# A 7-product (Strassen) first matrix product over pairs of batches, with its weights streamed from DRAM

## The chip, the cores and the metric

The kernel runs on one core of a Trainium2 chip. A core has a matrix engine (TensorE, `PE` in the profile, with its weight loads as `PEld`), three engines for element-wise work (VectorE `DVE`, ScalarE `ACT`, GpSimd `POOL`) and a sync engine (`SP`) that issues the transfers between DRAM and the on-chip memory SBUF. Matmuls write to PSUM, a second on-chip memory of eight banks. The metric is the device time of one execution in microseconds (us). Before the change the median of three runs was 1854.67 us (1854.55 to 1856.01).

## What is computed

Attention with RMS-normalised queries and keys over 8 batches, 12 heads, 448 positions and 64 columns a head, and behind it a feed-forward layer whose activation is the square of a Relu:

```
q_n, k_n = rmsnorm(q, g_q), rmsnorm(k, g_k)
scores = (1/sqrt(64)) * q_n @ k_n^T
attn = exp(scores - max); attn = attn / (sum(attn) + 1e-9)
x = (attn @ v), heads side by side        # 3584 x 768
h = x @ w_in                              # 768 x 2048
out = relu(h)^2 @ w_out                   # 2048 x 768
```

Inputs q, k, v and the gains are taken as f32. The weights arrive as 64-bit floats; the kernel itself turns their words into f32.

## The kernel before

The kernel has two versions of the work behind a test on the gains; the one with bounded scores (no row maximum), `attention_then_ffn_bounded`, runs here.

**Attention** goes by pairs of heads, 6 pairs a batch, 48 in all. For pair i, `load` and `load_v` (L414, L421) bring q, k and v into SBUF, `norm` (L429) squares on GpSimd (L434), reduces on VectorE (L437), takes the power -1/2 on GpSimd (L439) and scales (L441). `transposes` (L448) turns q and k on TensorE into `pt`, two PSUM tiles of the pool `ps_m`, and VectorE copies them out with the gains (L456). `scores` (L459) makes one of four chunks of keys: two matmuls, one per head, on halves of the array, then an exponential on ScalarE (L468); GpSimd adds the four chunks' probabilities up (L472, L474). `values` (L478) multiplies by v into `pav`; `finish` (L487) forms the row sums `tot` by a matmul with ones (L492), takes the reciprocal on VectorE (L494) and scales `pav` into the tile `xT` (L497).

**Feed-forward** of one batch (`feed_forward`, L506) has 16 row blocks of the first product, each six matmuls `ph` over the 768 inner rows (L513), a Relu on ScalarE (L516) and a square on GpSimd (L517) into `gT`; and then the second product, 128 rows of output at a time, in two halves of 384 columns, each 16 matmuls `po` (L525), copied out by VectorE (L528) or ScalarE (L530) and stored by SP (L533, L535). `ps_m` has two banks, which `pt`, `ph` and `po` share; `pav` and `tot` have one each, the scores four.

**The weights** `w1` and `w2` lie in SBUF throughout. They come in 32 pieces of 128x768, three in flight; `round_weights` (L392) makes f32 of each with five VectorE operations (L402, L404, L405, L407, L408), two on ScalarE (L403, L406) and a product on GpSimd (L409). Raw words and scratch lie in `gT`.

**The order.** The main loop (L560 to L596) goes over the batches; each batch's attention has twelve half-pairs, and after each half-pair some yields of the feed-forward of the batch before are run, so that TensorE has work of both. Batch 0 has no feed-forward to weave in; its half-pairs take the weight pieces instead. The last feed-forward runs alone. TensorE's instructions keep the order in which the program writes them (L635); the other engines' and SP's order is set by the planner, which works with estimated durations. An f32 matmul appears as two records in the profile.

## Time and profile before

| what | value |
|---|---|
| median of three runs | 1854.67 us |
| the profiled execution, its own time | 1852.34 us |
| its span, first to last instruction | 1850.5 us |
| TensorE busy | 1624.2 us (88%) |
| VectorE, ScalarE, GpSimd busy | 496.7, 304.4, 833.4 us |
| mean granted TensorE clock | 0.944 of full speed |
| moved by DMA | 70.16 MB, 38 GB/s on average |

The page cuts the span into 40 slices of 46 us and gives the busy share of an engine in tenths (9 is 90% or more). A table of windows gives the same for chosen stretches. A row of the timeline or of the groups names the line, the operation, output and inputs, partitions x elements, and a count; in a group, `| busy us, mean ns | idle us before it`, with the releaser that ended most of the idle time behind `<-`. The busy time of VectorE and GpSimd includes time in which an instruction has started and is held up.

### The profile page before, as it was taken

What the parts mean: (1) busy time and instruction counts of PE and PEld (TensorE: products, weight loads), DVE (VectorE), ACT (ScalarE), POOL (GpSimd) and SP (SyncE); (2) the same over time, 40 slices, a digit from 0 to 9 for tenths busy, and PEclk for the clock granted to TensorE, in tenths of its full rate; (3) what the DMA queues carried; (4) which work ended last, traced back from release to release, by engine and by line L of the source; (5) the groups of instructions that cost most, each with busy time, mean ns of one, the idle gap of its engine ahead of it and who ended that gap; (6) DMA issues with size and microseconds to landing.
All of it is one profiled execution on the core that took longest, in us unless ns stands there. A gap on an engine that the chain in (4) does not pass through costs nothing.

```text
span 1850.5 us, 13250 instructions
## 1 busy us (share of the span) xinstructions
PE 1624.2 (88%) x5440; PEld 804.5 (43%) x5440; DVE 496.7 (27%) x432; ACT 304.4 (16%) x413; POOL 833.4 (45%) x553
## 2 busy tenths in 40 slices
PE   3242479998999899998999899998999899999998
PEld 1111134454445444454445454454445454455555
DVE  6898941211211211211211212211211212210000
ACT  2333322101120011201120011201120011200100
POOL 6777676622662236622662236622663235601200
PEclk9657679998999999999999999999999999999999
DMA  5433400000100100000100100000100100000000
GB/s 157 135 119 116 148 25 25 20 33 24 30 25 24 37 24 21 25 33 24 30 26 24 37 24 17 29 32 24 30 25 24 37 24 15 10 18 9 0 10 27
DMA packets 47754, 70.16 MB, mean 38 GB/s; under 512 B 3652, under 2 KB 35908, under 8 KB 47684
## 3 DMA queue, kind: packets, MB, share of 16 engines
q1 hardware_dynamic: 47684, 69.22, 12.0%
q8 instruction: 44, 0.72, 0.2%
q14 instruction: 26, 0.21, 0.0%
HBM read 58.20 MB, written 11.01 MB: 37 GB/s over the span
## 4 chain that ended last, share of the span: by engine, by line
PE 81%; POOL 4%; DVE 2%; ACT 1%; issue 0%; POOLq 0%; ACTq 0%
PE po L525 32%; PE ph L513 32%; PE sc L465 7%; PE pav L484 6%; PE tot L492 2%; POOL acc L474 2%; PE pt L454 1%; POOL rstd L439 1%; ACT gT L516 1%; POOL qkn L441 1%; POOL qkn L434 1%; DVE rstd L437 0%; DVE w L407 0%; ACT osb L530 0%; DVE w L408 0%
## 5 line engine op out<-in xcount | busy, mean ns | idle before, releaser
L513 PE MATMUL ph<-xT,w 128*128 128x448 f32 x1536 | 595.6, 544 | 7.6 <-DVE xT L497 7.6
L525 PE MATMUL po<-w,gT 128*128 128x384 f32 x1792 | 592.3, 492 | 0.0
L525 PEld LDWEIGHTS po<-w,gT 128*128 128x128 f32 x1792 | 342.5, 192 | 256.0 <-issue 27.5
L513 PEld LDWEIGHTS ph<-xT,w 128*128 128x128 f32 x1536 | 287.5, 190 | 314.1 <-issue 305.6
L494 DVE RECIPROCAL rec<-tot 128x448 f32<-128x448 f32 x48 | 141.9, 2956 | 554.5 <-PE tot L492 554.5
L517 POOL TENSOR_TENSOR gT<-gT 128x448 f32<-128x448 f32 x128 | 118.3, 933 | 293.9 <-ACT gT L516 293.9
L465 PE MATMUL sc<-qkT 64*112 64x448 f32 x768 | 188.5, 614 | 60.1 <-DVE qkT L456 60.1
L472 POOL TENSOR_TENSOR acc<-pr 112x896 f32<-112x896 f32 x48 | 102.8, 2141 | 287.3 <-ACT pr L468 287.1
L474 POOL TENSOR_TENSOR acc<-acc,pr 112x896 f32<-112x896 f32 x96 | 201.1, 2095 | 27.5 <-ACT pr L468 27.1
L468 ACT ACTIVATE pr<-sc 112x896 f32<-112x896 f32 x192 | 166.9, 913 | 157.5 <-PE sc L465 157.5
L434 POOL TENSOR_TENSOR qkn<-qk 112x1024 f32<-112x1024 f32 x48 | 91.5, 1907 | 201.9 <-PE pt L454 191.7
L516 ACT ACTIVATE gT<-ph 128x448 f32<-128x448 f32 x128 | 69.7, 544 | 596.4 <-PE ph L513 596.4
L484 PE MATMUL pav<-pr,vt 112*64 112x448 f32 x768 | 167.4, 561 | 0.0
L456 DVE TENSOR_SCALAR qkT<-pt,gains 128x448 f32<-128x448 f32 x96 | 65.3, 682 | 340.0 <-PE pt L454 338.9
L454 PE MATMUL pt<-ident,qkn 112*128 112x112 f32 x384 | 62.1, 289 | 98.0 <-POOL qkn L441 88.5
L439 POOL TENSOR_TENSOR rstd<-rstd,mhalf 112x16 f32<-112x16 f32 x48 | 139.7, 2911 | 3.8
L465 PEld LDWEIGHTS sc<-qkT 64*112 64x112 f32 x768 | 67.1, 189 | 141.8 <-issue 133.5
L530 ACT COPY osb<-po 128x384 f32<-128x384 f32 x28 | 13.4, 479 | 682.3 <-PE po L525 682.3
L528 DVE COPY osb<-po 128x384 f32<-128x384 f32 x28 | 15.6, 558 | 349.2 <-PE po L525 349.2
L441 POOL TENSOR_TENSOR qkn<-qk,rstd 112x512 f32<-112x512 f32 x96 | 101.7, 1063 | 3.6
L454 PEld LDWEIGHTS pt<-ident,qkn 112*128 112x128 f32 x384 | 45.3, 153 | 132.2 <-POOL qkn L441 83.0
L484 PEld LDWEIGHTS pav<-pr,vt 112*64 112x64 f32 x768 | 48.3, 139 | 115.1 <-issue 90.2
(27 smaller groups left out, 497.4 us busy)
## 6 DMA issues: line engine op xcount, KB each, us to landing
gT<-in_moe_w_in_dram SPq DMA_DIRECT2D x16, 768.0 KB, 4.8
gT<-in_moe_w_out_dram SPq DMA_DIRECT2D x16, 768.0 KB, 4.3
qk<-in_q_dram SPq DMA_DIRECT2D x48, 224.0 KB, 2.9
qk<-in_k_dram SPq DMA_DIRECT2D x48, 224.0 KB, 3.2
vt<-in_v_dram SPq DMA_DIRECT2D x48, 224.0 KB, 2.7
out_dram<-osb SPq DMA_DIRECT2D x24, 384.0 KB, 2.3
out_dram<-osb SPq DMA_DIRECT2D x8, 192.0 KB, 2.7
gains<-in_g_q_dram SPq DMA_DIRECT2D x2, 0.2 KB, 2.9
```

The lines of the kernel that those rows point to most:

```text
L434: nc.gpsimd.tensor_tensor(sq, flat, flat, ALU.mult)
L439: nc.gpsimd.tensor_tensor(rflat, rflat, mhalf, ALU.pow)
L441: nc.gpsimd.tensor_tensor(qkn[:, s].rearrange("p j h d -> p h j d"), qk[:, s].rearrange("p h (j d) -> p h j d", d=D), rstd[:, s].rearrange ...
L454: nc.tensor.transpose(pt[:, j * SP:(j + 1) * SP], qkn[:, s, j].rearrange("p h d -> p (h d)"), ident[:SP, :SP])
L465: nc.tensor.matmul(sc[:, h, 0:S], qkT[rows, 1, c * SP:(c + 1) * SP], qkT[rows, 0, :], start=True, stop=True)
L468: nc.scalar.activation(pr, sc[:, :, 0:S], AF.Exp)
L474: nc.gpsimd.tensor_tensor(accs[i], accs[i], pr, ALU.add)
L484: nc.tensor.matmul(pavs[i][h * D:(h + 1) * D, :], vs[i][:, h, c, :], pr[:, h, :], start=(c == 0), stop=(c == NJ - 1))
L494: nc.vector.reciprocal(rec, tot)
L513: nc.tensor.matmul(ph, w1[:, c, f * P:(f + 1) * P], xT[:, c, :], start=(c == 0), stop=(c == NPAIR - 1))
L517: nc.gpsimd.tensor_tensor(g, g, g, ALU.mult)
L525: nc.tensor.matmul(po, gT[:, f, c0 + t:c0 + t + P], w2[:, f, cols], start=(f == 0), stop=(f == NFC - 1))
```

## The change

Attention itself keeps its shape; the feed-forward now takes two batches (896 rows) at a time, four such *spans*.

- **First product.** The 2 x 2 block product (inner halves of 384, row blocks f and f + 8 of the 2048, the two batches) is made with seven block products in place of eight (`first_product`). The seven combinations of weight blocks of each f are computed once, on GpSimd, and stored in a DRAM tile `w1s`; in each span they are loaded again, 192 KB each, six buffers, five products ahead (`load_blocks`). The combinations of the inputs are made by VectorE in `finish` (`xC`, and part of `xT`). Seven products are combined through PSUM accumulation (`pa`, `pd`, `pc` are each reopened once) and VectorE additions.
- **Second product.** It goes over 896 rows in seven tiles, yields after every matmul, and takes the 16 blocks in an order that leaves the last written ones to the end.
- **Order.** Head: attention of batches 0 and 1 with the conversion of w_in (`make_w1`). Then, four times, the first product alone, and the second product woven with the attention of the next two batches. w_out is converted (`make_w2`) during the first of the first products.
- **Conversion.** One `min` moves from VectorE to ScalarE: three VectorE operations and an exponent step, three on ScalarE; the fraction's words are overwritten in place.
- **Attention.** The square moves to ScalarE, and so does the evacuation of `pt`; in the head the row sums come from TensorE chunk by chunk (`pe_sums`) with no additions; later one of three additions is on VectorE.
- **SP** now keeps the written order too.

```diff
+    HC = NPAIR // 2
+    HF = NFC // 2
+    NSPAN = B // 2
...
+    gT = consts.tile([P, NFC, 2 * S], F32, name="gT")
+    xT = consts.tile([P, 2, NPAIR, S], F32, name="xT")
+    xC = consts.tile([P, 3, HC, S], F32, name="xC")
+    clamp1 = consts.tile([P, 1], F32, name="clamp1")
...
+    def exponents(words, w):
+        wu = w.bitcast(U32)
+        nc.vector.tensor_scalar(wu, pairs_of(words)[1], 20, 0x7FF, ALU.logical_shift_right, ALU.bitwise_and)
+        nc.scalar.activation(w, wu, AF.Relu, bias=clamp1, scale=-1.0)
+        nc.scalar.activation(wu, w, AF.Relu, bias=clamp2, scale=-(2.0 ** 23))
+    def fractions(words, w):
+        low, high = pairs_of(words)
+        wu = w.bitcast(U32)
+        f = low.bitcast(F32)
+        nc.vector.scalar_tensor_tensor(wu, high, 0x80000000, wu, ALU.bitwise_and, ALU.bitwise_or)
+        nc.vector.tensor_scalar(high, high, 0xFFFFF, None, ALU.bitwise_and)
+        nc.vector.scalar_tensor_tensor(f, low, 2.0 ** -32, high, ALU.mult, ALU.add)
+        nc.scalar.activation(f, f, AF.Copy, bias=1.0, scale=2.0 ** -20)
...
+    w1s = dram.tile([HF, 7, P, HC * P], F32, name="w1s")
+    SETS = 3
...
+    def make_w1(n, step):
+        if not 0 <= n < NFC:
+        b = [w1_blocks(n)[:, i] for i in range(8)]
+        at = (S2, A22)[n % 2]
+        e = w1_blocks(n)[:, at:at + 2].rearrange("p k m -> p (k m)")
+        words = w1_words(n)
+        A21 = 7
+        if step == 0 and doubles:
+            exponents(words, e)
+        if step == 1 and doubles:
+            fractions(words, e)
+        if step == 2:
+            for half, blk in enumerate(((A11, A12), (A21, A22))[n % 2]):
+                part = slice(half * HC * P, (half + 1) * HC * P)
+                if doubles:
+                    nc.gpsimd.tensor_tensor(b[blk], pairs_of(words)[0].bitcast(F32)[:, part], e[:, part], ALU.mult)
+                else:
+                    nc.gpsimd.tensor_copy(b[blk], words.bitcast(F32)[:, part])
+            load_w1(n + SETS)
+        if step == 2 and n % 2:
+            nc.gpsimd.tensor_tensor(b[S1], b[A21], b[A22], ALU.add)
+            nc.gpsimd.tensor_tensor(b[S2], b[S1], b[A11], ALU.subtract)
+            nc.gpsimd.tensor_tensor(b[S3], b[A11], b[A21], ALU.subtract)
+            nc.gpsimd.tensor_tensor(b[S4], b[A12], b[S2], ALU.subtract)
+        if step == 3 and n % 2:
+            nc.sync.dma_start(w1s[n // 2].rearrange("k p m -> p k m"), w1_blocks(n)[:, 0:7])
...
+    def w2_words(n):
+        f = (HF - 2, NFC - 2, HF - 4)[n % SETS]
+        return gT[:, f:f + 2, :].rearrange("p f n -> p (f n)")[:, 0:2 * NW].bitcast(U32)
...
+    def make_w2(n, step):
+        if not 0 <= n < NFC:
+            return
+        if step == 0 and doubles:
+            exponents(w2_words(n), w2[:, n])
+        if step == 1 and doubles:
+            fractions(w2_words(n), w2[:, n])
+        if step == 2:
+            if doubles:
+                f = pairs_of(w2_words(n))[0].bitcast(F32)
+                nc.gpsimd.tensor_tensor(w2[:, n], f, w2[:, n], ALU.mult)
+            load_w2(n + SETS)
+    stream = []
+    def load_blocks(upto):
+        while len(stream) < min(upto, NSPAN * HF * 7):
+            n = len(stream)
+            sw = loads.tile([P, HC, P], F32, tag="sw", name="sw", bufs=6)
+            nc.sync.dma_start(sw.rearrange("p c m -> p (c m)"), w1s[n // 7 % HF, n % 7])
+            stream.append(sw)
...
     def norm(i):
         qk = qks.pop(i)
...
-        nc.gpsimd.tensor_tensor(sq, flat, flat, ALU.mult)
+        nc.scalar.activation(sq, flat, AF.Square)
...
     def transposes(i):
         qkn = normed.pop(i)
...
-            nc.vector.tensor_scalar(qkT[:, s], pt, gains[:, s:s + 1], None, ALU.mult)
+            nc.scalar.activation(qkT[:, s], pt, AF.Copy, scale=gains[:, s:s + 1])
...
         probs[i, c] = pr
-        if c == 1:
+        if c == 0 or pe_sums:
+            pass
+        elif c == 1:
             accs[i] = work.tile([SP, 2, S], F32, tag="acc", name="acc")
             nc.gpsimd.tensor_tensor(accs[i], probs[i, 0], pr, ALU.add)
-        elif c > 1:
-            nc.gpsimd.tensor_tensor(accs[i], accs[i], pr, ALU.add)
+        else:
+            (nc.vector if c == 2 else nc.gpsimd).tensor_tensor(accs[i], accs[i], pr, ALU.add)
         if c == NJ - 1:
             del qkTs[i]
-    def values(i, cs):
+    def values(i, cs, pe_sums):
...
             for h in range(2):
                 nc.tensor.matmul(pavs[i][h * D:(h + 1) * D, :], vs[i][:, h, c, :], pr[:, h, :],
                                  start=(c == 0), stop=(c == NJ - 1))
-    def finish(i):
+            if pe_sums:
+                sums(i, pr, c == 0, c == NJ - 1)
+        if not pe_sums and NJ - 1 in cs:
+            sums(i, accs.pop(i), True, True)
+    def sums(i, pr, first, last):
+        if first:
+            tots[i] = ps_o.tile([P, S], F32, tag="t", name="tot")
+        for h in range(2):
+            nc.tensor.matmul(tots[i][h * D:(h + 1) * D, :], ones, pr[:, h, :], start=first, stop=last)
+    def finish(work, i):
         b, hp = divmod(i, NPAIR)
-        acc = accs.pop(i)
-        tot = ps_o.tile([P, S], F32, tag="t", name="tot")
-        for h in range(2):
-            nc.tensor.matmul(tot[h * D:(h + 1) * D, :], ones, acc[:, h, :], start=True, stop=True)
+        t = b % 2
         rec = work.tile([P, S], F32, tag="rec", name="rec", bufs=1)
-        nc.vector.reciprocal(rec, tot)
-        if hp == 0:
-            xTs[b] = work.tile([P, NPAIR, S], F32, tag="xT", name="xT")
-        nc.vector.tensor_tensor(xTs[b][:, hp, :].rearrange("d (p j) -> d j p", j=NJ),
+        nc.vector.reciprocal(rec, tots.pop(i))
+        nc.vector.tensor_tensor(xT[:, t, hp, :].rearrange("d (p j) -> d j p", j=NJ),
                                 pavs.pop(i).rearrange("d (j p) -> d j p", j=NJ),
                                 rec.rearrange("d (j p) -> d j p", j=NJ), ALU.mult)
         del vs[i]
+        if t:
+            sub = nc.vector.tensor_tensor
+            if hp < HC:
+                sub(xC[:, 0, hp], xT[:, 1, hp], xT[:, 0, hp], ALU.subtract)
+            else:
+                n = hp - HC
+                sub(xC[:, 1, n], xT[:, 1, hp], xC[:, 0, n], ALU.subtract)
+                sub(xC[:, 2, n], xT[:, 0, hp], xC[:, 1, n], ALU.subtract)
+                sub(xT[:, 1, n], xT[:, 1, hp], xT[:, 1, n], ALU.subtract)
+    def attention(work, span, pe_sums):
+        first, end = 2 * span * NPAIR, 2 * (span + 1) * NPAIR
+        for i in range(first, end):
+            if i + 2 < B * NPAIR:
+                load(i + 2)
+            scores(work, i, 0, pe_sums)
+            scores(work, i, 1, pe_sums)
+            if i + 1 < end:
+                norm(i + 1)
+            if i > first:
+                values(i - 1, (2, 3), pe_sums)
+                finish(work, i - 1)
+            yield
+            if i + 1 < B * NPAIR:
+                load_v(i + 1)
+            if i + 1 < end:
+                transposes(i + 1)
+            scores(work, i, 2, pe_sums)
+            scores(work, i, 3, pe_sums)
+            values(i, (0, 1), pe_sums)
+            if i == end - 1:
+                values(i, (2, 3), pe_sums)
+                finish(work, i)
+            yield
+    def first_product(work, span):
+        B11, B21, B22 = xT[:, 0, 0:HC], xT[:, 0, HC:], xT[:, 1, HC:]
+        T1, T2, T4, T3 = xC[:, 0], xC[:, 1], xC[:, 2], xT[:, 1, 0:HC]
+        def product(ps, n, rhs, first):
+            load_blocks(n + 6)
+            for c in range(HC):
+                nc.tensor.matmul(ps, stream[n][:, c], rhs[:, c], start=first and c == 0,
+                                 stop=c == HC - 1, skip_group_check=not first)
+        def activate(g, src):
+            nc.scalar.activation(g, src, AF.Relu)
+        for f in range(HF):
+            n = (span * HF + f) * 7
+            g11, g12 = gT[:, f, 0:S], gT[:, f, S:2 * S]
+            g21, g22 = gT[:, HF + f, 0:S], gT[:, HF + f, S:2 * S]
+            add = nc.vector.tensor_tensor
+            pa = ps_o.tile([P, S], F32, tag="t", name="pa")
+            product(pa, n + A11, B11, True)
+            p1 = work.tile([P, S], F32, tag="p1", name="p1")
+            nc.scalar.copy(p1, pa)
+            yield
+            pb = ps_m.tile([P, S], F32, tag="m", name="pb")
+            product(pb, n + S2, T2, True)
+            z = work.tile([P, S], F32, tag="z", name="z")
+            add(z, p1, pb, ALU.add)
+            yield
+            pc = ps_m.tile([P, S], F32, tag="m", name="pc")
+            product(pc, n + S1, T1, True)
+            y = work.tile([P, S], F32, tag="y", name="y")
+            add(y, z, pc, ALU.add)
+            yield
+            pd = ps_m.tile([P, S], F32, tag="m", name="pd")
+            product(pd, n + S3, T3, True)
+            add(g22, y, pd, ALU.add)
+            activate(g22, g22)
+            yield
+            product(pa, n + A12, B21, False)
+            activate(g11, pa)
+            yield
+            product(pd, n + A22, T4, False)
+            add(g21, z, pd, ALU.add)
+            activate(g21, g21)
+            yield
+            product(pc, n + S4, B22, False)
+            add(g12, z, pc, ALU.add)
+            activate(g12, g12)
+            yield
+    chunks = [f for f in range(NFC) if f % HF < HF - 1] + [HF - 1, NFC - 1]
+    def second_product(work, span):
+        for t in range(0, 2 * S, P):
             osb = work.tile([P, DM], F32, tag="osb", name="osb")
             for half in range(2):
                 cols = slice(half * HALF, (half + 1) * HALF)
                 po = ps_m.tile([P, HALF], F32, tag="m", name="po")
-                for f in range(NFC):
-                    nc.tensor.matmul(po, gT[:, f, c0 + t:c0 + t + P], w2[:, f, cols],
-                                     start=(f == 0), stop=(f == NFC - 1))
-                if half == 0:
-                    nc.vector.tensor_copy(osb[:, cols], po)
-                else:
-                    nc.scalar.copy(osb[:, cols], po)
-                if half == 1:
-                    if t < FULL:
-                        nc.sync.dma_start(out[b * S + t:b * S + t + P, :], osb)
-                    else:
-                        nc.sync.dma_start(out[b * S + FULL:(b + 1) * S, :], osb[0:REST])
-                        nc.sync.dma_start(out[(b - 1) * S + FULL:b * S, :], osb[REST:P])
-                yield
+                for f in chunks:
+                    nc.tensor.matmul(po, gT[:, f, t:t + P], w2[:, f, cols],
+                                     start=(f == chunks[0]), stop=(f == chunks[-1]))
+                    if f == chunks[-1]:
+                        if half == 0:
+                            nc.vector.tensor_copy(osb[:, cols], po)
+                        else:
+                            nc.scalar.copy(osb[:, cols], po)
+                            nc.sync.dma_start(out[2 * span * S + t:2 * span * S + t + P, :], osb)
+                    yield
...
+    NB = 4 * NPAIR
+    with tc.tile_pool(name="first", bufs=2, reuse_waits="tile") as work:
+        for u, _ in enumerate(attention(work, 0, True)):
+            for n in range((NFC + 3) * u // NB, (NFC + 3) * (u + 1) // NB):
+                for step in (3, 0, 1, 2):
+                    make_w1(n - step, step)
+    for n in range(SETS):
+        load_w2(n)
+    for span in range(NSPAN):
+        more = span + 1 < NSPAN
+        nxt = 2 * (span + 1) * NPAIR
+        with tc.tile_pool(name="first_product", bufs=2, reuse_waits="tile") as work:
+            for u, _ in enumerate(first_product(work, span)):
+                if span == 0:
+                    for n in range(4 * u // 7, 4 * (u + 1) // 7):
+                        for step in range(3):
+                            make_w2(n - step, step)
+                if more and u == 7 * (HF - 2):
+                    norm(nxt)
+                if more and u == 7 * (HF - 1):
+                    transposes(nxt)
+        with tc.tile_pool(name="second_product", bufs=2, reuse_waits="tile") as work:
+            rest = second_product(work, span)
+            if more:
+                each, done = (2 * S // P) * 2 * NFC - 24, 0
+                for u, _ in enumerate(attention(work, span + 1, False)):
+                    while done < each * (u + 1) // NB:
+                        next(rest)
+                        done += 1
+            load_blocks((span + 1) * HF * 7 + 6)
+            for _ in rest:
+                pass
...
     args = (q, k, v, g_q, g_k, w_in, w_out, out)
     with tc.If(bits <= limit) as small_scores:
-        with tc.manual_schedule(engines={mybir.EngineType.PE}):
+        with tc.manual_schedule(engines={mybir.EngineType.PE, mybir.EngineType.SP}):
             attention_then_ffn_bounded(tc, *args)
```

140 lines of the change are left out of this document (36 added, 104 removed).

## The prediction

> **What bounds the kernel now.** I read the page's slices first, then the table of windows, then the chain of waits, then single stretches of the timeline.
>
> ```profile
> span 1850.5 us, 13250 instructions
> PE   3242479998999899998999899998999899999998
> ```
>
> The first five slices (46 us each) differ from all others: TensorE is at most 0.4 busy there, and at 0.9 from slice 6 on. Two stretches of the table of windows (columns: length, then busy us with counts of PE, PEld, DVE, ACT, POOL, clock, DMA share, GB/s) and the two last pieces of the chain fix the sizes:
>
> ```profile
> 15.00:256.00 241.00, 94.71 (x308) 37.13 (x308) 211.31 (x196) 79.22 (x93) 175.88 (x90) 0.68 0.39 122
> 256.00:1690.00 1434.00, 1375.28 (x4688) 682.81 (x4687) 281.17 (x228) 214.41 (x301) 636.02 (x435) 0.98 0.08 25
> ...
> 1689.53 72.16 PE ph L513 x192
> 1761.69 82.57 PE po L525 x256
> ...
> 1844.33 0.48 ACT L530 COPY osb<-po 128x384 f32<-128x384 f32 x1 [20.16 <-PE po L525]
> ```
>
> So the span is four pieces: a head of 256 us (attention of batch 0 alone, with the conversion of all weights), 1434 us for seven batches of attention woven with the feed-forward of the batch before, 154.8 us of the last feed-forward alone, and 6.2 us from the last copy's start at 1844.33 to the end. In the head VectorE and GpSimd bind: 211.3 + 175.9 = 387 us of busy time in 241. In the seven batches TensorE binds; its steps there, one record being one pass and two records one f32 matmul:
>
> ```profile
> 446.39 1.76 PE L465 MATMUL sc<-qkT 64*112 64x448 f32 x8
> 448.09 9.29 PE L513 MATMUL ph<-xT,w 128*128 128x448 f32 x24
> 457.21 0.55 PE L454 MATMUL pt<-ident,qkn 112*128 112x112 f32 x4
> 458.01 0.60 PE L454 MATMUL pt<-ident,qkn 112*128 112x112 f32 x4 [0.25 <-ACT gT L516]
> 458.54 1.76 PE L465 MATMUL sc<-qkT 64*112 64x448 f32 x8
> 460.23 1.72 PE L484 MATMUL pav<-pr,vt 112*64 112x448 f32 x8
> 474.35 0.92 PE L492 MATMUL tot<-acc,ones 112*64 112x448 f32 x4
> ...
> 581.97 20.84 PE po L525 x64
> ```
>
> By starts, 24 `ph` records take 457.21 - 448.09 = 9.12 us, 0.380 each (0.376 in the 192 of the last stage); 64 `po` records take 20.84, 0.326 each (0.3225 in the last 256). Eight `sc` records take 1.69, eight `pav` 1.66, four `tot` 0.92, one pair's transposes 1.33. A head pair costs TensorE 2 x 1.69 + 2 x 1.66 + 0.92 + 1.33 = 8.95 us.
>
> **The change, stage by stage.** The new span is a head (attention of *two* batches with w_in's conversion), then four times a first product alone and a second product, three of the latter woven with attention of the next two batches.
>
> *First product.* Seven products of three matmuls replace eight: 4 spans x 8 x 7 x 3 x 2 = 1344 records for 1536. They run alone, like the last stage: 336 x 0.376 = 126.3 us per span. Per row block (15.8 us) there are four Relu and a copy on ScalarE, five VectorE additions out of PSUM and four squares on GpSimd:
>
> ```profile
> L516 ACT ACTIVATE gT<-ph 128x448 f32<-128x448 f32 x111 | 60.4, 544 | 528.9 <-PE ph L513 528.9
> L497 DVE TENSOR_TENSOR xT<-pav,rec 128x448 f32<-128x448 f32 x42 | 40.6, 966 | 1.5
> L517 POOL TENSOR_TENSOR gT<-gT 128x448 f32<-128x448 f32 x111 | 102.4, 933 | 213.2 <-ACT gT L516 213.2
> ```
>
> 5 x 0.54, 5 x 0.97 and 4 x 0.93, all under 5 us of 15.8: hidden. The added waits (a second accumulation into `pa`, `pc`, `pd` after the addition that read them) have one product, 2.26 us, between; no row shows a reopened group. Bounds: nothing, or 0.25 us each (the longest PSUM wait quoted below, L454 at 458.01) for 96, 24 us; below nothing is excluded, since nothing goes. I take 0.7 us per span: 127.
>
> *Streamed weights.* 224 loads of 192 KB, one per 2.26 us:
>
> ```profile
> gT<-in_moe_w_in_dram SPq DMA_DIRECT2D x16, 768.0 KB, 4.8
> qk<-in_k_dram SPq DMA_DIRECT2D x48, 224.0 KB, 3.2
> vt<-in_v_dram SPq DMA_DIRECT2D x48, 224.0 KB, 2.7
> ```
>
> The nearest rows are 224 KB in 2.7 to 3.2 us. Six buffers let five products (11.3 us) pass between issue and use, and 192 KB per 2.26 us is 87 GB/s where the 768 KB loads make 160. Hidden; cover gone, see the fourth rival. The eight stores of 1344 KB in the head are by the first row under 9 us each, beside 16 us pairs: hidden.
>
> *Second product with attention* (three times). Per span 448 `po` records x 0.327 = 146.5, and 12 pairs x 8.95 = 107.4. One new wait: the woven work now stops after any matmul, so a `po` accumulation stands open in one of the two banks of `ps_m` at each pair's transposes (done counts 8, 25, 41 ... are never multiples of 16). The second transpose group then waits until the first has been evacuated; the scores, values and all second-product matmuls queue behind it. The row L454 at 458.01 waits 0.25 us for a bank; the whole trip from transposes over an evacuation is this:
>
> ```profile
> 15.49 1.92 PE L454 MATMUL pt<-ident,qkn 112*128 112x112 f32 x8 [15.49 <-POOL qkn L441]
> ...
> 17.71 1.27 DVE L456 TENSOR_SCALAR qkT<-pt,gains 128x448 f32<-128x448 f32 x2
> ...
> 19.03 3.33 PE L465 MATMUL sc<-qkT 64*112 64x448 f32 x8 [1.62 <-DVE qkT L456]
> ```
>
> 17.41 to 17.71 to start, 0.64 for one of the two; with ScalarE's 0.54 (L516) about 0.9 us. Bounds 0.25 and 1.6 (both evacuations); I take 0.9, as the wait is for the group just written: 11 x 0.9 = 9.9 per span. At the end of each span the sums wait on the last additions, as now:
>
> ```profile
> PE tot L492 <- POOL acc L474: 49.2, 7, 7.9
> ```
>
> 49.2 / 7 = 7.0 us; now one of three additions is on VectorE and no norm is in GpSimd's way: 0 to 7, I take 4. Sum: 146.5 + 107.4 + 9.9 + 4 = 267.8. SP's written order puts the loads of q, k and v behind an output store that waits for its last copy; they are used a pair (22 us) later and land in 3.2, so this costs nothing, and 3.2 us a pair without that lead. Last second product: 448 x 0.3225 = 144.5.
>
> *Head.* The rows of uncontended and of blocked operations:
>
> ```profile
> 154.13 0.55 DVE L404 TENSOR_SCALAR gT<-gT 128x768 uint32<-128x768 uint32 x1
> 154.60 0.94 DVE L408 SCALAR_TENSOR_TENSOR w<-gT,w 128x768 uint32<-128x768 uint32 x1
> ...
> 222.50 2.39 POOL L409 TENSOR_TENSOR w<-gT,w 128x768 f32<-128x768 f32 x1 [1.43 <-DVE w L408]
> 223.15 2.16 DVE L407 TENSOR_SCALAR w<-w 128x768 uint32<-128x768 uint32 x1
> 226.91 1.80 POOL L409 TENSOR_TENSOR w<-gT,w 128x768 f32<-128x768 f32 x1 [2.02 <-DVE w L408]
> ...
> L468 ACT ACTIVATE pr<-sc 112x896 f32<-112x896 f32 x166 | 143.3, 914 | 98.5 <-PE sc L465 98.5
> L494 DVE RECIPROCAL rec<-tot 128x448 f32<-128x448 f32 x42 | 124.2, 2958 | 554.5 <-PE tot L492 554.5
> L439 POOL TENSOR_TENSOR rstd<-rstd,mhalf 112x16 f32<-112x16 f32 x40 | 116.4, 2910 | 3.3
> L441 POOL TENSOR_TENSOR qkn<-qk,rstd 112x512 f32<-112x512 f32 x80 | 83.4, 1042 | 3.1
> L437 DVE TENSOR_REDUCE rstd<-qkn 112x16 f32<-112x1024 f32 x40 | 48.8, 1220 | 58.9 <-POOL qkn L434 58.9
> L434 POOL TENSOR_TENSOR qkn<-qk 112x1024 f32<-112x1024 f32 x39 | 73.8, 1892 | 191.7 <-PE pt L454 191.7
> L474 POOL TENSOR_TENSOR acc<-acc,pr 112x896 f32<-112x896 f32 x84 | 174.3, 2075 | 24.0 <-ACT pr L468 23.9
> ```
>
> Per w_in piece VectorE does two shifts or masks at 0.55 (L404) and two combinations at 0.95: 3.0 us, the min (L407) having moved to ScalarE. Per pair (16 pieces for 12 pairs) that is 4.0, and 1.22 + 2.96 + 0.97 for reduce, reciprocal and scaling, and about 0.7 of new subtractions (0.55 to 0.97 each, from L408 by size and L497): 9.9. GpSimd: 2.91 + 2 x 1.04 for the norm, products of 384 columns at half of 1.80 = 0.9, 32 of them and 32 block sums in 12 pairs = 4.8: 9.8. The square and the three additions have left it. The dependent loop of one pair, with one `tot` and one `pav` bank: sums end, reciprocal and scaling 3.9 + 0.3, values with sums 3.4, scores 1.7, values with sums 3.4: 12.7. But GpSimd and VectorE hinder one another: L407, of the form of L404 (0.55), took 2.16 at 223.15: it began inside a GpSimd product (222.50 to 224.89) and ended 0.4 after it. In the present head the uncontended work is 32 x (3 x 0.55 + 2 x 0.95) + 6 x (1.22 + 2.96 + 0.97 + 1.27) = 152 on VectorE and 32 x 1.80 + 6 x (1.89 + 2.91 + 2 x 1.04 + 3 x 2.07) = 136 on GpSimd; the stretch of 241 is 0.84 of the two in sequence. The same share of 9.9 + 9.8 is 16.5 per pair. Between 12.7 and 16.5 I take 16, near the second, since it is measured (for the range 13 to 22): 15.5 of start (first transposes at 15.49) + 192 = 207.5. TensorE itself: the sums now take sixteen `tot` records a pair for four, 8.95 + 3 x 0.9 = 11.6 of the 16. Its clock is 0.68 in the present head, where it is busy 94.7 of 241; with 11.6 of 16 I expect more. [...]
>
> *The first first product* also converts w_out: 16 pieces within 32 products, 72 us. There VectorE has 16 x 3.0 + 4.6 x 5 x 0.97 = 70 us of work, GpSimd 16 x 1.8 + 4.6 x 4 x 0.93 = 46. Side by side both fit and the cost is nothing; if conversions and GpSimd exclude one another, 48 + 46 = 94, and 22 us stick out. The rows at 222.50 and 223.15 say the second. I take 20 (0 to 35), the waiting conversion holding first the `load_w2` behind it on SP, then the stream loads queued there. [...] Before it, the last pair's reciprocal, scaling and subtraction outlast the product that needs none of them: 4.9 - 2.26, 2.6. Together 127 + 20 + 2.6 = 149.6.
>
> *Sum.* 207.5 + 149.6 + 3 x 267.8 + 3 x 127 + 144.5 + 6.2 = 1692. The profiled execution's time was 1852.3 for a span of 1850.5, and the median of three is 1854.7, 4.2 above the span: **1696 us**. Of the 158 us gained, 73 come from 192 records less and about 85 from the head, whose conversion of w_out moves under a stage that TensorE fills.
>
> **Rivals.** *All hides:* pairs at 12.7, no excess, 0.25 per transpose, nothing at the span ends: 1696 - 40 - 20 - 21 - 12 = **1603**. For it: rows of uncontended work; against it, the blocked ones. *The head stays a chain of queues:* in the present head TensorE stood behind evacuations and norms that were late:
>
> ```profile
> PE pt L454 <- POOL qkn L441: 88.5, 11, 15.5
> PE sc L465 <- DVE qkT L456: 60.1, 6, 15.5
> ```
>
> 148.6 us over six pairs, 25 each. A third of that on top of 16 makes 24 us per pair: + 96, **1792**. Against it: the evacuation moves to ScalarE, which has some 9 us of work per pair (four exponentials at 0.91, and by their columns 1.0 for the square, 1.1 for two evacuations, 3.3 for conversions). *Only the products count:* the head gains nothing, 1854.7 - 73 = **1782**; it lies beside the former. *The stream is serial, the slower case:* if SP, in written order, had one load in flight, each product would take the 3.2 us of the k load: 224 x (3.2 - 2.26) = 211, **1907**. From 2.97 us per load on (159 / 224 more) there is no gain. Against it, three 768 KB loads issued together at the start, and buffers for five:
>
> ```profile
> 9.09 1.52 SPq L390 DMA_DIRECT2D gT<-in_moe_w_in_dram  x3
> ```
>
> That the change does not cut the products is excluded by their count in the code.
>
> **Chances.** Forecast 0.60; all hides 0.17; head a queue or no gain in it 0.19; serial stream 0.04. The range reaches towards both neighbours without holding their ends: 1625 to 1775, which takes in 13 to 22 us per pair, and the bounds of the excess and of the transposes. A difference of 0.2% is about what a measurement tells from none. Faster 0.95, same 0.01, slower 0.04.
>
> **What would show it.** Right: first product's first record near 207 us; granted clock in the head above 0.8; spans of 127 us with TensorE at 1.0; 33 waits of `pt` near 0.9 on ScalarE; in the first first product, VectorE conversions above 0.55 and 0.95. Wrong: waits of TensorE on the stream loads; a head above 250; `tot` waits on additions in every pair.

## The result, and the profile after

The changed kernel takes 1669.8 us (median of 4 runs, 1668.06 to 1671.21) beside 1855.3 for the kernel before: a ratio of 0.900, 95% interval 0.8984 to 0.9015. It is faster, as forecast; the forecast of 1696 us was 26 us too high. The profiled execution took 1669.05 us for a span of 1667.2. Its page's first slices, to be read against the five slow slices of before:

```profile
span 1667.2 us, 14210 instructions
...
PE 1556.5 (93%) x5392; PEld 771.7 (46%) x5392; DVE 550.1 (33%) x548; ACT 452.5 (27%) x621; POOL 659.1 (40%) x482
...
PE   5768788899999999999999999999999999999998
...
PEclk9989999999999999999999999999999999999999
...
sw<-w1s SPq DMA_DIRECT2D x224, 192.0 KB, 2.4
```

TensorE reaches 0.9 in slice 9 (42 us each), later than before, but the slices ahead of it hold two batches' attention and a whole first product instead of one batch's attention. The table of windows by stage (columns as in the prediction: length, busy us and counts of PE, PEld, DVE, ACT, POOL, then clock, DMA share, GB/s), for the head, the first first product, the first woven second product, the second first product; and the last stage, from the chain:

```profile
15.00:210.50 195.50, 146.92 (x672) 58.22 (x672) 125.65 (x110) 109.11 (x134) 145.65 (x114) 0.90 0.54 175
210.50:360.70 150.20, 135.87 (x346) 66.37 (x346) 91.93 (x107) 63.20 (x88) 69.73 (x51) 0.96 0.44 141
360.70:618.70 258.00, 249.31 (x969) 123.17 (x969) 84.03 (x67) 67.92 (x88) 115.74 (x70) 1.00 0.14 42
618.70:746.50 127.80, 127.35 (x345) 64.42 (x343) 25.36 (x40) 24.35 (x43) 33.94 (x35) 1.00 0.31 89
```
```profile
1516.84 144.49 PE po L690 x448
```

Where the 183.3 us of the two spans' difference (1850.5 - 1667.2) came from: TensorE's busy time fell by 67.7 (1624.2 to 1556.5) and its idle time by 115.6. The idle time of before was 146.3 in the head's window and 58.7 in the seven batches; now it is 48.6 in the head, 14.3 in the first first product and 8.7 in each woven stage. What TensorE still waits for, in the whole span (columns: us in total, times, longest):

```profile
PE pav L566 <- issue: 38.5, 11, 5.2
PE pt L534 <- ACT qkT L536: 24.2, 33, 0.8
PE pt L534 <- POOL qkn L521: 21.3, 5, 15.7
PE pd L636 <- DVE z L656: 9.7, 4, 4.3
PE pd L636 <- DVE gT L665: 3.4, 2, 2.8
PE pa L636 <- DVE rec L585: 3.1, 1, 3.1
PE tot L577 <- POOL acc L556: 1.8, 3, 0.6
```

`issue` stands for time in which the profile shows nothing that the engine waited for. In the first row it is the one bank of `pav`: in the three such waits between 85 and 125 us the values begin 0.1 us after VectorE's scaling of the pair before, which reads that bank, has ended. One of them:

```profile
107.17 0.94 DVE L586 TENSOR_TENSOR xT<-pav,rec 128x448 f32<-128x448 f32 x1
108.20 0.97 PE L566 MATMUL pav<-pr,vt 112*64 112x448 f32 x4 [2.43 <-issue]
```

No wait for a streamed load is among the rows: the 192 KB land 2.4 us after their issue (median), with five products of 2.26 us between issue and use.

### The profile page after: what moved, and what is told of

The parts are those of the page before. It is cut to its first block, busy times and chain, and to the rows that moved or that the text cites. A ratio compares the mean times of both kernels' runs of the same rounds, so it can differ in the third digit from the quotient of the medians.

```text
span 1667.2 us, 14210 instructions
## 1 busy us (share of the span) xinstructions
PE 1556.5 (93%) x5392; PEld 771.7 (46%) x5392; DVE 550.1 (33%) x548; ACT 452.5 (27%) x621; POOL 659.1 (40%) x482
## 4 chain that ended last, share of the span: by engine, by line
PE 84%; DVE 4%; POOL 3%; issue 3%; ACT 3%; DMA 2%; SPq 0%; DVEq 0%; POOLq 0%; ACTq 0%
PE po L690 36%; PE sc L545 8%; PE pav L566 8%; PE pd L636 8%; PE pc L636 8%; PE pa L636 7%; PE pb L636 4%; PE tot L577 3%; PE pt L534 2%; ACT qkT L536 1%; DMA w1s<-gT 1%; POOL gT L450 1%; DVE gT L400 1%; POOL rstd L519 1%; DVE gT L401 1%
## 5 line engine op out<-in xcount | busy, mean ns | idle before, releaser
L566 PE MATMUL pav<-pr,vt 112*64 112x448 f32 x768 | 177.2, 572 | 38.5 <-issue 38.5
L545 PE MATMUL sc<-qkT 64*112 64x448 f32 x768 | 172.2, 568 | 0.7 <-ACT qkT L536 0.7
L518 POOL TENSOR_SCALAR rstd<-rstd 112x16 f32<-112x16 f32 x48 | 37.6, 784 | 321.4 <-DVE rstd L517 320.5
L636 PE MATMUL pa<-xT,sw 128*128 128x448 f32 x384 | 156.8, 545 | 3.1 <-DVE rec L585 3.1
L640 ACT ACTIVATE gT<-gT 128x448 f32<-128x448 f32 x96 | 55.2, 575 | 302.8 <-DVE gT L665 183.2
L536 ACT ACTIVATE qkT<-pt,gains 128x448 f32<-128x448 f32 x96 | 59.4, 632 | 276.2 <-PE pt L534 276.2
L517 DVE TENSOR_REDUCE rstd<-qkn 112x16 f32<-112x1024 f32 x48 | 58.2, 1212 | 186.3 <-ACT qkn L514 186.0
L636 PEld LDWEIGHTS pa<-xT,sw 128*128 128x128 f32 x384 | 74.0, 193 | 76.0 <-issue 71.2
L534 PE MATMUL pt<-ident,qkn 112*128 112x112 f32 x384 | 55.1, 271 | 45.6 <-ACT qkT L536 24.2
L636 PE MATMUL pd<-xT,sw 128*128 128x448 f32 x192 | 80.1, 554 | 9.7 <-DVE z L656 9.7
L556 POOL TENSOR_TENSOR acc<-acc,pr 112x896 f32<-112x896 f32 x36 | 75.0, 2084 | 33.7 <-DVE acc L556 33.7
L554 POOL TENSOR_TENSOR acc<-pr 112x896 f32<-112x896 f32 x36 | 74.9, 2081 | 28.7 <-ACT pr L548 28.7
```

The lines of the kernel that those rows point to most:

```text
L534: nc.tensor.transpose(pt[:, j * SP:(j + 1) * SP], qkn[:, s, j].rearrange("p h d -> p (h d)"), ident[:SP, :SP])
L536: nc.scalar.activation(qkT[:, s], pt, AF.Copy, scale=gains[:, s:s + 1])
L545: nc.tensor.matmul(sc[:, h, 0:S], qkT[rows, 1, c * SP:(c + 1) * SP], qkT[rows, 0, :], start=True, stop=True)
L556: (nc.vector if c == 2 else nc.gpsimd).tensor_tensor(accs[i], accs[i], pr, ALU.add)
L566: nc.tensor.matmul(pavs[i][h * D:(h + 1) * D, :], vs[i][:, h, c, :], pr[:, h, :], start=(c == 0), stop=(c == NJ - 1))
L636: nc.tensor.matmul(ps, stream[n][:, c], rhs[:, c], start=first and c == 0, stop=c == HC - 1, skip_group_check=not first)
```

## The experiments

The theory was the prediction's: 192 records less, a head set by VectorE and GpSimd together, an excess in the first first product from the conversion of w_out, 11 bank waits per woven stage. Rivals: the gain has little to do with the count of products; the head is set by the dependent loop of one pair; the stream, or SP's written order, decides. Stage times below run from a stage's first matmul to the next one's, in the profiled execution.

**1. Eight products instead of seven,** streamed in the same way, summed in PSUM. (In this variant one piece of w_out is converted from words that the first product has by then overwritten: its values differ, the work and its time don't.)

```
-            nc.sync.dma_start(sw..., w1s[n // 7 % HF, n % 7])
+            nc.sync.dma_start(sw..., w1s[n // 4 % HF, (A11, A12, 7, A22)[n % 4]])
...
+            for r in range(2):
+                n = (span * HF + f) * 4 + 2 * r
+                for t in range(2):
+                    ps = ps_m.tile([P, S], F32, tag="m", name="ps")
+                    for half in range(2):
+                        for c in range(HC):
+                            nc.tensor.matmul(ps, stream[n + half][:, c], xT[:, t, half * HC + c], ...)
+                    activate(gT[:, r * HF + f, t * S:(t + 1) * S], ps)
```

> Eight block products for seven, each accumulated in PSUM and read by the Relu directly, with the same head, stream (four blocks per row block, each used twice) and weave. If the products' count is worth its records: 192 records of 0.376 more, +72 us, less up to 15 us in the first first product, where VectorE's 22 us of additions fall away: 1727 to 1742. If the additions and the stream give the saved products back: within 15 us of the changed kernel's 1670.

Measured: 1731.77 us (ratio 0.9347, 0.9332 to 0.9361), 62 more than the change. The later first products take 145.8 us for 127.8: 18 each, 48 records of 0.376. The first one takes only 157.9 for 150.2: 12 over the later ones of its kind, where the change has 22.4. It has no additions for the conversion to delay; what waits there is three products, 7.7 us together, for a late Relu on ScalarE. So 3 x 18 + 8 = 62 is what seven products for eight are worth, and the rest of the gain, some 123 us, has nothing to do with their count. No run divides these 123 between the head and the weave.

**2. No conversion** of weights (w_in's blocks hold a constant, and w_out's tiles are filled by loads of other f32 data, half the bytes; all else stays).

```
-        if step == 0 and doubles:
-            exponents(words, e)
-        if step == 1 and doubles:
-            fractions(words, e)
...
```

> Leaves out the conversion of both weights (VectorE, ScalarE and GpSimd operations on them; their transfers stay, w_out's from other memory). If conversion and the shared use of VectorE and GpSimd set the pace: the head's 195 us after the first transposes fall to some 168 (12.7 to 14 us per pair for 16.3), and the first first product from 150 to 129. If the loop over the one bank of pav and tot sets the head: it stays above 185. If the stream or the reopened groups cost the first first product its excess: it stays near 150.

Measured: 1628.64 us in one run. Its windows, head and first first product:

```profile
15.00:189.60 174.60, 140.29 (x673) 56.03 (x673) 63.44 (x45) 65.93 (x84) 62.88 (x50) 0.94 0.59 190
189.60:320.50 130.90, 130.46 (x344) 65.74 (x344) 27.98 (x44) 23.86 (x42) 33.94 (x35) 0.98 0.39 123
```
```profile
PE pav L544 <- issue: 26.7, 11, 2.4
```

The conversion costs 20.9 us in the head and 19.3 in the first first product. In the head VectorE's and GpSimd's busy times together fell from 271 to 126 us, and the pair only from 16.0 to 14.3. What is left is the dependent loop: the eleven waits at `pav` stay, each now 2.4 us, where the longest was 5.2. So both theories of the head are at work, one just above the other. The 20.9 compare one execution with one, and the head moves by some us by itself (see the end); and ScalarE lost its steps of the conversion too (109.1 to 65.9 us busy), so that run 3 is the one that loads VectorE and GpSimd alone.

**3. More work for GpSimd and VectorE in the head:** the row sums there by additions, as in the woven stages.

```
-        for u, _ in enumerate(attention(work, 0, True)):
+        for u, _ in enumerate(attention(work, 0, False)):
```

> In the head the row sums come again from additions on GpSimd and VectorE, as in the later spans, and one matmul group. If VectorE and GpSimd in sequence set the head's pace: 4.2 + 1.1 us more per pair at 0.84, +45 to +55, 1715 to 1725. If TensorE's loop sets it: within 15 us of the changed kernel, as TensorE gets 2.7 us less.

Measured: 1714.6 us (0.9251, 0.9237 to 0.9265), 45 more; the head takes 257.6.

```profile
PE tot L577 <- POOL acc L556: 48.3, 12, 9.9
```
```profile
257.63 4.41 PE L636 MATMUL pa<-xT,sw 128*128 128x448 f32 x6 [8.72 <-DMA sw<-w1s]
```

24 additions on GpSimd at 2.08 us and 12 on VectorE at 1.08, as undisturbed in the later stages, are 63 us of work. 47 come back by the start of the first product. 6 of these are a wait for the first streamed block, 8.7 us where the wait for the reciprocal was 3.05: SP, in written order, issues that load behind the last store of `w1s`, which GpSimd's last block sum held until 245.5. The other 41 lie ahead of the head's last record, though TensorE does fewer sums. Work added on these two engines is paid at two thirds of its length; what run 2 took away there (16 pieces at 3.0 on VectorE, 64 products and sums at 0.9 on GpSimd: 106 us undisturbed) gave 20.9, a fifth.

**4. The other order of the loop in the head:** the last pair's values and `finish` ahead of the next scores.

```
+            if i > first and pe_sums:
+                values(i - 1, (2, 3), pe_sums)
+                finish(work, i - 1)
             scores(work, i, 0, pe_sums)
             scores(work, i, 1, pe_sums)
             if i + 1 < end:
                 norm(i + 1)
-            if i > first:
+            if i > first and not pe_sums:
```

> In the head alone, the last values and the finish of a pair stand before the next pair's first scores, so that 4.4 us of TensorE work lie between the end of the sums and the next use of the pav bank, where 2.7 did. If the loop over that bank sets the head: most of the eleven waits at pav (2.4 to 4.7 us) go, 15 to 28 us less, 1642 to 1655. If VectorE and GpSimd, at 0.84 of their summed work, set it: less than 5 us.

Measured: 1660.44 us (0.8955, 0.8942 to 0.8967), 9.4 less, between the two expectations. The waits at `pav` are gone and others stand in their place:

```profile
PE pt L534 <- POOL qkn L521: 36.7, 13, 15.6
PE sc L545 <- ACT pr L548: 12.6, 4, 9.3
PE pav L566 <- DVE xT L586: 2.0, 3, 1.3
```

With the loop shortened, the norms on GpSimd and the exponentials on ScalarE are late next. So in the head the loop (14.3 a pair by run 2) and the engines' queues (15.4 here) lie close to one another, and neither theory holds alone.

**5. SP ordered by the planner,** as before the change.

```
-        with tc.manual_schedule(engines={mybir.EngineType.PE, mybir.EngineType.SP}):
+        with tc.manual_schedule(engines={mybir.EngineType.PE}):
```

> SP's order is left to the planner, as in the kernel before; TensorE keeps the written one. If SP's order is not where the gain comes from: within 10 us of 1670. If the written order is what keeps the stream ahead of the products: waits of TensorE on stream loads, 30 us and more slower.

Measured: 1699.37 us (0.9163, 0.9149 to 0.9177), 29.6 more, which neither expectation had. The table of windows for the product that ends w_out's conversion (L480), head and first first product, first of the changed kernel and then of this one:

```profile
15.00:210.50 195.50, 0.00 (x0) 0.90 0.54 175
210.50:360.70 150.20, 31.87 (x16) 0.96 0.44 141
```
```profile
15.00:263.60 248.60, 30.23 (x15) 0.81 0.55 182
263.60:393.30 129.70, 1.85 (x1) 0.99 0.30 87
```

The planner issues the loads of w_out from 27.9 us on instead of from 195.6, and 15 of the 16 pieces are converted in the head. That head is 53 us longer, and the first first product 20.5 shorter (129.7). The stream is as before: no product waits for it. In the head it is the waits at `pav` that grew, 78.5 us for 38.5, while those for norms stay (22.2 for 21.3). So SP's written order is worth 30 us here, not through the stream but by keeping a conversion out of the stage whose engines have no room for it. It is also the cleanest sight of the excess: without the conversion beside it, the first first product is 129.7.

**6. The conversion of w_out at a lower rate.** The excess could be one of rate (VectorE gets behind) or of each late addition. A first try used two sets of words instead of three over 42 products; there a piece's exponents are taken from the words of a piece that came before, so that it changed more than the rate.

```
-        f = (HF - 2, NFC - 2, HF - 4)[n % SETS]
+        f = (HF - 2, NFC - 2)[n % 2]
...
-                    for n in range(4 * u // 7, 4 * (u + 1) // 7):
+                    for n in range(3 * u // 7, 3 * (u + 1) // 7):
```

> w_out's 16 pieces are converted over 42 products of the first first product for 32, with two sets of words. If VectorE and GpSimd are short of time in those 32 products (94 us of work that cannot overlap in 72): now 99 in 95, and the excess of 24 falls to 5 to 12, 12 to 18 us less, 1652 to 1658. If the excess comes from single late additions behind a conversion, whatever the rate: less than 5 us.

Measured: 1673.44 us (0.9014, 0.8999 to 0.9029), no gain; 148.8 in the stage. The second try keeps three sets, the third in a tile of its own:

```
+        if n % SETS == 2:
+            return spares[0]
+        f = (HF - 2, NFC - 2)[n % SETS]
...
+                spares.append(work.tile([P, 2 * NW], U32, name="spare", bufs=1))
...
+                    for n in range(3 * u // 7, 3 * (u + 1) // 7):
```

> The conversion of w_out is spread over 42 of the 56 products of the first span instead of 32 (three pieces per seven products for four), and the third set of words lies in a tile of its own, since g's tiles are written that far on; all three sets stay, so every piece is converted from its own words. In the changed kernel the first span's product takes 150.2 us beside 126.3 to 127.9 in the others: some 23 us lost to the conversion. If they are lost because VectorE has too much to do at that rate (queues build up), they fall by more than half: 10 us or less are left and the kernel takes 1654 to 1661 us. If each late addition costs the same wherever it falls (one piece ahead of an addition on VectorE, a TensorE wait, some matmuls at half clock behind it), 18 to 24 us are left and the time stays within 1664 to 1672 us.

Measured: 1678.02 us (1669.7 to 1680.22; 0.9028, 0.9009 to 0.9048), and 151.7 in the stage, 23.8 over the later ones: a rate lower by a quarter takes nothing off. The time lies outside both expectations, because the head of this execution, whose code is the change's but for the first loads of w_out, began the first product at 220.2 instead of 210.5. How the loss arises can be read in the changed kernel's first first product. VectorE's steps there, and three of the products that waited for an addition (timeline: start, us, and in brackets the idle time before):

```profile
L389 DVE TENSOR_SCALAR w<-gT 128x768 uint32<-128x768 uint32 x15 | 11.9, 795 | 1.9 <-DMA gT<-in_moe_w_out_dram 1.9
L399 DVE SCALAR_TENSOR_TENSOR w<-gT,w 128x768 uint32<-128x768 uint32 x16 | 17.4, 1089 | 6.3 <-ACT w L392 6.2
L400 DVE TENSOR_SCALAR gT<-gT 128x768 uint32<-128x768 uint32 x16 | 19.5, 1216 | 0.2
L401 DVE SCALAR_TENSOR_TENSOR gT<-gT 128x768 f32<-128x768 uint32 x16 | 20.4, 1276 | 1.1
```
```profile
220.63 2.52 PE L636 MATMUL pd<-xT,sw 128*128 128x448 f32 x6 [1.68 <-DVE z L656]
...
263.68 3.99 PE L636 MATMUL pd<-xC,sw 128*128 128x448 f32 x6 [2.79 <-DVE gT L665]
...
299.81 4.85 PE L636 MATMUL pd<-xT,sw 128*128 128x448 f32 x6 [4.34 <-DVE z L656]
```

L400 takes 1.22 us where its form takes 0.55 undisturbed, L401 1.28 for 0.95. The four steps of a piece make 4.4 us by these means, where 3.0 is undisturbed. An addition caught behind them comes late, and the product that needs its bank waits: seven times, 13.7 us together (0.58 to 4.34). This is what stood ahead of the last of the three:

```profile
293.89 1.68 DVE L399 SCALAR_TENSOR_TENSOR w<-gT,w 128x768 uint32<-128x768 uint32 x1
295.61 2.08 DVE L400 TENSOR_SCALAR gT<-gT 128x768 uint32<-128x768 uint32 x1
...
299.14 0.61 DVE L656 TENSOR_TENSOR z<-p,pb 128x448 f32<-128x448 f32 x1
```
```profile
295.00 2.27 POOL L480 TENSOR_TENSOR w<-gT,w 128x768 f32<-128x768 f32 x1 [0.24 <-ACT gT L402]
```

The inputs of the addition `z` were there at 295.4. L400 began inside GpSimd's product (295.00 to 297.27) and ended 0.4 us after it, two more steps of the conversion followed, and the addition began at 299.14. Behind waits of 1.63 to 2.10 the six records take 2.52 us at a granted clock of 1.00; behind 2.79 and 4.34 they take 3.99 and 4.85 at a clock that falls to 0.50: with the product behind each, another 4.5. So slowed, with the one behind the 3.05 us at `pa` (3.93, another 1.5), are three products of six records each, not six products, as the expectation for one buffer below has it. Waits and slowed records make 19.7 of the 22.4 us.

**7. The depth of the stream:** two buffers and one, instead of six.

```
-            sw = loads.tile([P, HC, P], F32, tag="sw", name="sw", bufs=6)
+            sw = loads.tile([P, HC, P], F32, tag="sw", name="sw", bufs=2)
...
-            load_blocks(n + 6)
+            load_blocks(n + 2)
```

> Two stream buffers for six, loads issued one product ahead. If a load's way of 2.4 us and its issue are what six buffers hide: 2.7 to 3.0 us of load against 2.26 of product, 0.45 to 0.75 of wait in each of 224 products, +100 to +170 us, 1770 to 1840. If loads land early enough whatever the depth: no difference.

> One buffer for the streamed blocks: each product's load is issued when the product before it has read its weights. The price of a stream that hides nothing, which was the slower rival of the forecast: the product's 2.26 us, and 2.4 us from issue to landing with some 0.3 us for the two hand-overs, 4.9 to 5.1 us per product, 2.65 to 2.85 us more for each of 224: 590 to 640 us more, 2260 to 2310 us in all. If a wait of some 2.7 us also halves the clock of the matmuls behind it, as waits of 1.7 to 4.3 us did for six products in the first span of the changed kernel (3.9 to 4.85 us for 2.25), the product takes 6.5 to 7.5 us and the kernel 2620 to 2850 us.

Measured with two: 1731.74 us (0.9334, 0.9318 to 0.9349), 62 more, which neither expectation had. A first product takes 13 to 15 us longer, 0.25 per product. A load is issued when the product before last has read its buffer, so it has one product's 2.26 us, and 2.51 is what issue, landing (2.3) and hand-over take; the expectation had 2.7 to 3.0.

With one: 2557.77 us, in one run. Its waits, the window of the first first product, and three products:

```profile
PE pd L636 <- DMA sw<-w1s: 157.5, 64, 2.6
PE pc L636 <- DMA sw<-w1s: 153.5, 63, 2.8
PE pa L636 <- DMA sw<-w1s: 144.9, 59, 2.6
PE pb L636 <- DMA sw<-w1s: 76.9, 32, 3.3
```
```profile
213.30:567.10 353.80, 219.12 (x344) 85.36 (x344) 78.38 (x107) 64.52 (x88) 63.79 (x51) 0.75 0.20 63
```
```profile
412.74 4.82 PE L636 MATMUL pd<-xT,sw 128*128 128x448 f32 x6 [2.48 <-DMA sw<-w1s]
420.06 2.49 PE L636 MATMUL pa<-xT,sw 128*128 128x448 f32 x6 [2.50 <-DMA sw<-w1s]
424.99 4.19 PE L636 MATMUL pd<-xC,sw 128*128 128x448 f32 x6 [2.44 <-DMA sw<-w1s]
```

The 218 listed waits are 2.4 us each, as from two buffers (2.5). Of the three products the first takes 4.82 us behind a wait of 2.48, the second 2.49 behind 2.50; at full clock it is 2.26 to 2.52. TensorE's busy time for the product's 336 records and the few others went from 135.9 to 219.1 us, at a granted clock of 0.75: 6.3 us per product, 2.26 + 2.44 + some 1.6 for the clock. With load and product taking turns the stream costs 888 us. The prediction's slower rival was another case, one load in flight beside the running product, at 211 us; two buffers come nearest to it, at 62.

**8. Two matmuls between the transposes** in the woven stages, so that the second group does not wait for the first one's evacuation.

```
-                transposes(i + 1)
+                transposes(i + 1, (0,))
+                yield False
+                transposes(i + 1, (1,))
...
-                    while done < each * (u + 1) // NB:
+                    while done < each * u // NB + (0 if main else 2):
```

> Two matmuls of the second product are put between the two transpose groups of a pair in the weave; nothing else moves. If the wait for the one free bank is a loss of its own: 33 x 0.73 to 0.82, 24 to 27 us less, 1643 to 1646. If it is only moved to another wait (scores behind the later evacuation): less than 8 us.

Measured: 1658.04 us (0.8942, 0.893 to 0.8954), 11.8 less, between the two expectations. The 24.2 us of `pt` waits are gone, the three woven stages take 15.7 us less (253.0 for 258.0 in the first; the head of this execution was 9.6 us longer, with the same code), and this stands where 1.8 us stood:

```profile
PE tot L578 <- POOL acc L557: 10.8, 26, 0.6
```

The two matmuls were taken from the stretch that covered the additions for the sums.

**9. Together:** runs 4 and 8, and two matmuls ahead of the sums. And the same with run 6's lower rate.

```
                 values(i - 1, (2, 3), pe_sums)
+                yield False
+                sums(i - 1, accs.pop(i - 1), True, True)
                 finish(work, i - 1)
```

> Three things together: two second-product matmuls between the two groups of transposes in the woven spans; two more of them ahead of the sums over the keys there, which take the additions on GpSimd; and in the head the values of the last pair and its finish ahead of the scores of the next. The first alone gave 11.8 us and gave some 9 us back to waits of tot for acc; the third alone gave 9.4. If the parts add up and the waits of tot go, 12 + 9 + 9 = 30 us: 1635 to 1645 us, with woven spans of 250 us for 258. Rival: the finish comes later, and the wait moves on to pav, which waits for the reciprocal: 1646 to 1655 us, with spans of 253.

> e_all2 with the slower conversion of w_out (42 products for 32). It differs from e_all2 by what that edit gives by itself: -8 to -15 us if the loss in the first span is one of rate (1622 to 1636 us), within 4 us of e_all2 if every late addition costs the same.

Measured: 1641.35 us (1639.31 to 1643.29; 0.8846, 0.8834 to 0.8858), 28 less than the change, as the first expectation had it; with the lower rate 1644.87 (0.887, 0.8857 to 0.8882), 3.5 more, as the second one had it if every late addition costs the same. The woven stage has no idle time left:

```profile
354.50:605.90 251.40, 251.34 (x969) 120.66 (x969) 84.06 (x67) 67.72 (x88) 115.20 (x70) 1.00 0.14 43
```

Of the 10.8 us listed at `tot` in run 8, 4.0 came off the stages (758.3 to 754.3 for the three); TensorE's busy time in the first rose from 249.2 to 251.3 instead. So part of a listed wait was not idle time to be won: it came back as TensorE's busy time.

## Why the prediction was right, step by step

By terms, against the profiled execution's span:

| term | predicted | measured |
|---|---|---|
| head, to the end of its last record | 207.5 | 207.5 |
| first first product, with the wait before it | 149.6 | 153.2 |
| three woven second products | 803.4 | 774.0 |
| three later first products | 381 | 382.0 |
| last second product | 144.5 | 144.6 |
| tail | 6.2 | 5.9 |
| sum | 1692 | 1667.2 |

- **Fewer records** came as counted (0.376 each, run 1). The bound of 24 us for reopened groups was not needed: the later first products take 126.3 to 127.9.
- **The woven stages** hold the error: 9.8 us each. 4.6 is the sum itself: the last pair of a stage has no transposes (1.33), the row for transposes already held the 0.25 us wait that 0.9 was to stand for (11 x 0.25 = 2.75), and 0.5 stays unassigned. Another 3.4 is the wait of the sums at a stage's end, 0.62 us where 4 was taken between 0 and 7, and 1.8 the bank wait, 0.73 for 0.9. The bank wait itself was there as foretold, 33 times; what was foretold of `tot` in every pair as a sign of error appeared only when run 8 took its cover.
- **The head** came out at 16.0 us a pair as taken, its reason half right; that the size was hit is in part luck. VectorE with GpSimd set it (run 3, and the 53 us of run 5), but the loop of a pair lies at 14.3 (run 2), not 12.7, so the sum of the two engines is not the only limit. It also moves by itself: in the profiled executions of other kernels with the same head code the first product began at 213.3 to 220.1 instead of 210.5, up to 16.8 a pair. TensorE was busy 12.2 us a pair there (146.9 in twelve), at a granted clock of 0.90, where 11.6 had been counted.
- **The first first product**: the 20 us for engines that exclude one another are 19.3 (run 2) and 20.5 (run 5). The engines do hold each other up (L400 took 1.22 us for 0.55, L401 1.28 for 0.95); that they exclude one another altogether was the author's assumption, and no run shows it. And the place was wrong: not the loads behind a waiting conversion, but late additions, and a clock of 0.50 behind the waits for two of them (2.79 and 4.34 us). And that 94 - 72 = 22 us of work without room gave the size is luck: over 42 products there are 95 us of room, and the excess stayed at 23.8 (run 6). The wait before it was 3.05 for 2.6, and 1.4 us of slow clock behind it.
- **The stream** was hidden, as said; what its cover is worth is run 7.
- **A reading**: slice 6 of before is at 0.7, not 0.9, and the slices behind it at 0.8 or 0.9. No term rests on it; the sum took the windows.
- *Rivals.* All hides: no; even without conversion a pair takes 14.3, not its 12.7. Queues in the head, only the products: no; the products are a third of the gain. Serial stream: no, with two buffers it would still have been 0.9334 of before.

## What to carry to other kernels

When an operand stream replaces a resident one, work out what the depth at hand covers: with k buffers a load has k - 1 steps to land. Two buffers, just too few, cost 0.25 us per product here; one cost 4, of which 2.44 is waiting and some 1.6 went with a granted clock of 0.75. The head, in which two engines share the load and a loop is close behind, charged two thirds of the work added (41 of 63 us, run 3) and paid back a fifth of the work removed (20.9 of 106, run 2), so keep deferrable work (and the loads that release it) out of such a stage, in the written order if the planner would pull it in. And when a bubble is filled by moving matmuls, look at what those matmuls covered before.

## What the runs showed of the hardware

- The granted clock of TensorE fell behind some waits of 2.4 to 4.3 us and not behind others, so the length of the wait alone did not decide it. In the first first product it stayed at 1.00 behind single waits of 1.63 to 2.10 us; it was 0.50 from 264.6 to 268.0, behind a wait of 2.79, and from 298.6 to 305.5, around one of 4.34. With one buffer, where a wait of some 2.44 us stood before every product, it was 0.75 on average: the product behind a wait of 2.50 took 2.49 us, the next, behind 2.44, took 4.19.
- The executions of this kernel, whose head TensorE fills by three quarters (146.9 of 195.5 us), differ from one another. Five executions of the kernel with the lower rate (run 6) took 1669.7 and 1671.8 us at a mean granted clock of 0.984 and 0.985, and 1678.0 to 1680.2 at 0.977 to 0.979. In four kernels with the same head code (the change, one buffer, two buffers, run 8) the granted clock in the profiled head was 0.90, 0.91, 0.88 and 0.85, with TensorE's busy time there at 146.9, 147.7, 153.7 and 154.7 us and the first product's start at 210.5, 213.3, 219.5 and 220.1.
- Streamed loads of 192 KB landed in 2.3 to 2.4 us at the median, with six buffers, two or one. The slowest of a run took 4.7 to 8.9 us (8.7 in the changed kernel); the first one of run 3, issued behind the last store of `w1s` and three loads of w_out, took 8.2.
